# Later w1 loads, routing numbers in a PSUM bank and two more unsplit heads in a fused attention and mixture-of-experts kernel

## The chip, the cores and the metric

The kernel runs on one core of one Trainium2 chip. Its time is the device time of one execution in microseconds (us), lower is better. One execution was also taken by the hardware profiler; every row below comes from that one. The engines are TensorE (PE in the rows, PEld for its weight loads), VectorE (DVE), ScalarE (ACT), GpSimd (POOL) and the queue of SyncE (SPq), which issues most transfers.

## The reference, cut to what matters

Causal attention over 4 batches, 12 heads, 448 positions and head size 64 gives 1792 rows of 768 numbers; a router picks the best of 8 experts for each row, and that expert's two matrices are applied.

```python
scores = scale * np.matmul(q, k.transpose(0, 1, 3, 2))        # 4 x 12 x 448 x 448, causal mask
attn = softmax(scores); x = np.matmul(attn, v)                # x: 1792 x 768 after the heads are joined
logits = x @ w_gate + modality_bias[modality_id]              # 1792 x 8
e_idx = np.argmax(logits, axis=1)
gate_w = (exp(l) / (sum(exp(l)) + 1e-9))[e_idx]               # l = logits - their maximum
for e in range(8):
    out[mask_e] = gate_w[mask_e, None] * (relu(x[mask_e] @ w1[e]) @ w2[e])
```

## The kernel before

The program is written out in one order for all engines; each engine runs its own instructions in that order, and semaphores hold an instruction until what it needs is done. Attention is a loop `iteration(n)` over 48 heads (n = 0 to 47; 12 heads of a batch in three groups of 4), software-pipelined: iteration n computes the scores of head n on TensorE (`st_scores`), then transposes the probabilities of head n-2 (`st_trans`), then multiplies those of head n-3 with v (`st_pv`, into the PSUM bank `ot`), then joins a quarter of a finished group (`st_comb`, into the bank `x`). VectorE takes row minima and copies the scores (`p`, L274), computes the low half of the split probabilities (`pl`, L315), adds the two halves of the product (`ut`, L359) and normalises (L406, L416). ScalarE takes the exponentials (L284), the high half (`ph`, L314) and the low rows of the product (`hol`, L353).

Matrix products in full precision are made of fp32r products of high and low parts. For q and k the split is GpSimd's: `split_qk` (L191, L192) and `split_kl` (L197, L199) for a pair of heads, two heads at a time, and `stack_qk` has four transfers bring the parts on top of each other in a tile `st`. Heads 0 to 3 do without: `first_load` loads q and k of a pair into the tiles `raw1`, and `st_scores` multiplies them unsplit in fp32 (half as many matmuls, each of them slower). `raw1` is later the place where the first expert's w1 lands. GpSimd also splits v for each group (`split_vh`, `split_vl`, L238 and L243).

When the last group of a batch is normalised, `after_batch(b, n)` puts the router's small steps of that batch into the next iterations: the six steps `choose` (logits, maximum, difference, ties, choice), `places` (seven small matmuls, then two ScalarE copies, the second the exponential of the differences), the steps `rank`, and `scatter`, GpSimd's four indirect writes of the row numbers. `later(n, f)` puts f behind the scores of iteration n, `before(n, f)` ahead of them, and `soon(n, f)` behind the transposes. The batches end at iterations 19, 31, 43 and in the tail, so `choose` stands in iterations 20 to 23, 32 to 35, 44 to 47 and in the tail.

After batch 1 the most frequent expert is taken as the first one to be computed (`first_expert`, `first_slot`); its w1 is loaded in six chunks, chunk k in iteration 31 + `W1AT[k]`. GpSimd splits chunks 0 to 2 in iterations 45, 46 and 47. The experts follow after the attention; TensorE bounds that part almost alone.

In the names of PSUM tiles each bank is 128 x 512 fp32; of bank `ot` the attention uses columns 0 to 447.

Of the kernel before, what the change touches and what calls it, by code (L numbers as in the profile page):

```python
# [21 lines left out]
def attention_moe(  # L22
# [47 lines left out]
    ps = ctx.enter_context(tc.tile_pool(name="ps", bufs=1, space=PSUM))  # L70

    def bank(tag, bufs=1):
        return ps.tile([128, 512], F32, tag=tag, name=tag, bufs=bufs)

    def sm(shape, tag, dt=F32, bufs=2):
        return small.tile(shape, dt, tag=tag, name=tag, bufs=bufs)

    def cst(name, shape, dt=F32):
        return const.tile(shape, dt, name=name)
# [16 lines left out]
    lts = [ltp[:, j] for j in range(2)]  # L96
    sls = [cst(f"sl{j}", [128, NTL, E + 1]) for j in range(2)]
    ent = cst("ent", [128, B, NTL, 2], I32)
# [119 lines left out]
    def first_view(m, c):  # L218
        return raw1[3 * m + c][:, 0:S]

# [214 lines left out]
    def route(b):  # L435
        lg = sm([128, NTL, E], "lg")
        m = sm([128, NTL], "m")
        eq = sm([128, NTL, E], "eq")
        m2 = sm([128, NTL], "m2")
        oh = sm([128, NTL, E], "oh", BF16)  # L440
        pe = sm([128, NTL, E], "pe")
        pc = sm([128, NP + E], "pc")
# [23 lines left out]
        def places():  # L466
            prev = rt[b - 1][0][:, NP:] if b else ebase
            ohf = oh.rearrange("p t e -> p (t e)")
            pos = bank("x")
            nc.tensor.matmul(  # L470
                pos[:, 0:NP + E].rearrange("p (t e) -> p t e", e=E), lhsT=onesf,
                rhs=eb(prev, NTL + 1)[0:1], start=True, stop=False,
            )
            nc.tensor.matmul(pos[:, 0:NP], lhsT=upper, rhs=ohf, start=False, stop=False)
            for j in range(1, NTL + 1):
                nc.tensor.matmul(
                    pos[:, j * E:NP + E], lhsT=ones, rhs=ohf[:, 0:NP + E - j * E], start=False, stop=(j == NTL)
                )
            A.activation(out=pc, in_=pos[:, 0:NP + E], func=AF.Copy)
            A.activation(out=pe, in_=lg, func=AF.Exp)  # L480
            rt[b] = (pc, si)
# [7 lines left out]
        def ranks():  # L489
            V.tensor_reduce(out=sr, in_=sl, axis=AX, op=ALU.add)  # L490
            V.tensor_scalar(out=zs, in0=zs, scalar1=1e-9, scalar2=None, op0=ALU.add)

        def gates():
            V.tensor_copy(si, sr)
            V.reciprocal(out=ent[:, b, :, 1].bitcast(F32), in_=zs)
# [7 lines left out]

        sr = sm([128, NTL], "sr")
        return (logits, top, centre, ties, first_tie, choice), places, (slots, ranks, gates), scatter

    def eb(a, x):
        return a.rearrange("p (o e) -> p o e", o=1).to_broadcast([a.shape[0], x, E])
# [26 lines left out]
    def first_base():  # L535
        V.tensor_scalar(out=eboff, in0=ebneg, scalar1=now[:, 2:3], scalar2=None, op0=ALU.add)
        V.tensor_scalar(out=eb64, in0=ebneg, scalar1=now[:, 3:4], scalar2=None, op0=ALU.add)

# [17 lines left out]
    def first_tri():  # L556
        V.tensor_scalar(out=n0, in0=oh0, scalar1=-1.0, scalar2=1.0, op0=ALU.mult, op1=ALU.add)
        V.tensor_tensor(out=tri0, in0=ctri, in1=eb(n0, E), op=ALU.mult)

    def first_order():  # L560
        V.tensor_tensor(out=tri0, in0=tri0, in1=eb(oh0, E), op=ALU.add)
        V.tensor_tensor(out=tri0, in0=tri0, in1=n0.rearrange("p (e o) -> p e o", o=1).to_broadcast([128, E, E]), op=ALU.mult)

# [309 lines left out]
    with tc.manual_schedule():  # L873
        for m in range(2):
            first_load(m)
        load_v(0)
        load_qk(2)
        nc.sync.dma_start(out=modi, in_=mod)
# [10 lines left out]
        V.memset(warm, 0.0)  # L889
        for m in range(2):  # L890
            for a in range(2):
                V.memset(first_view(m, a)[64 - a * 64:128 - a * 64], 0.0)
        A.activation(out=warm, in_=warm, func=AF.Exp)
# [34 lines left out]
        for j in range(2):  # L928
            V.memset(sls[j], 0.0)
            V.memset(sls[j][64:128, 0, E:E + 1], 1.0e6)  # L930
            V.memset(lts[j][64:128, 0], 0.0)
# [68 lines left out]
        e0 = []  # L1000
        W1AT = (8, 9, 14, 14, 15, 15)

# [8 lines left out]
        def after_batch(b, n):  # L1011
# [6 lines left out]
            last = b == B - 2  # L1018
            soon(n + 4, places)
            for j, f in enumerate(rank, 1):  # L1020
                (later if j % 2 else before)(n + 5 + j // 2, f)
            for i in range(NTL):
# [42 lines left out]
        def iteration(n):  # L1065
            if n % 2 == 1 and n + 3 < NHEAD:
                stack_qk((n + 3) // 2)
            if n and n % GH == 0 and n // GH + 1 < B * NG:
                load_v(n // GH + 1)
# [18 lines left out]
            if n == 0:  # L1088
                split_vh(0)
                split_vl(0)  # L1090
                load_v(1)
            if n % 2 == 1 and n + 3 < NHEAD:
                split_kl((n + 3) // 2)
            if n % 2 == 0 and n + 4 < NHEAD:
                split_qk((n + 4) // 2)
# [310 lines left out]
```

## Time and profile before

| | |
|---|---|
| median of 3 runs | 507.45 us (507.43 to 509.28) |
| the profiled execution | 509.06 us, of it span 507.3 us |
| TensorE busy | 478.0 us (94%) |
| VectorE, ScalarE, GpSimd busy | 302.1, 279.4, 242.8 us |
| mean granted TensorE clock | 0.990 of full speed |
| attention (scores of heads 0 to 47) | about 4 to 204 us of the span |

The span runs from the first instruction to the last; the 1.8 us around it belong to the execution too. Busy time over the whole span mixes the attention, in which four engines are busy nearly all the time, with the experts, in which TensorE alone is.

### The profile page before, as it was taken

To read this page: it belongs to the slowest core of one execution; us is meant where nothing else is said; L and a number is where in the kernel's file an instruction comes from. 1 tells how busy PE (TensorE), PEld (TensorE's weight loads), DVE (VectorE), ACT (ScalarE), POOL (GpSimd) and SP (SyncE) were. 2 spreads that over 40 slices of the span, in tenths; PEclk is the share of its full clock that TensorE was granted. 3 is DMA by queue.
4 is the path that set the end of the run, shared out by engine and by line. 5 is a ranking of instruction groups with operands and counts; after the bars stand their busy time and mean duration, and the time that the engine had idled before them with its cause. 6 is when DMAs were issued, how large, how long until landed. Compare 5 with 4: busy or idle time off the path is not lost.

```text
span 507.3 us, 10362 instructions
## 1 busy us (share of the span) xinstructions
PE 478.0 (94%) x3359; PEld 442.8 (87%) x3359; DVE 302.1 (60%) x893; ACT 279.3 (55%) x690; POOL 242.8 (48%) x295
## 2 busy tenths in 40 slices
PE   8699999999989988899999999999999999999990
PEld 6589899899878977778999999999999999889770
DVE  7689888999899989888523015452021120184490
ACT  5499999899978977624322125442112211284670
POOL 5799999899999979952220202202101001021131
PEclk9899999999999999999999999999999999999997
DMA  5998788987997869765478300972101001076200
GB/s 149 210 237 212 181 229 239 285 223 188 243 263 222 199 124 270 248 164 71 96 265 328 96 32 21 323 281 66 63 1 54 31 2 64 31 261 214 88 14 6
DMA packets 44106, 79.84 MB, mean 157 GB/s; under 512 B 15614, under 2 KB 27646, under 8 KB 44032
## 3 DMA queue, kind: packets, MB, share of 16 engines
q1 hardware_dynamic: 40992, 67.98, 49.1%
q0 software_dynamic: 3040, 11.03, 6.3%
q8 instruction: 28, 0.46, 0.4%
q14 instruction: 46, 0.38, 0.2%
HBM read 48.10 MB, written 11.89 MB: 118 GB/s over the span
## 4 chain that ended last, share of the span: by engine, by line
PE 48%; POOL 16%; DVE 12%; DMA 11%; issue 6%; ACT 4%; SPq 1%; POOLq 0%; DVEq 0%; ACTq 0%
PE g L747 7%; PE g L748 7%; PE g L749 7%; DVE pl L315 3%; DVE p L274 2%; DMA table<-ent,si 2%; POOL hl L192 2%; DMA st<-hl 2%; POOL vhl L243 2%; PE ot L748 2%; PE ot L747 2%; PE x L749 2%; PE x L748 2%; PE x L747 2%; PE ot L749 2%
## 5 line engine op out<-in xcount | busy, mean ns | idle before, releaser
L284 ACT ACTIVATE p<-p,nm 128x448 f32<-128x448 f32 x192 | 94.8, 497 | 4.3 <-DVE nm L274 4.3
L728 POOL DMA_INDIRECT xg<-xs,idg x18 | 20.9, 1161 | 156.4 <-DVEq L1316 79.3
L766 DVE SCALAR_TENSOR_TENSOR htl<-g,hth 128x256 fp32r<-128x256 f32 x40 | 16.7, 424 | 103.8 <-ACT hth L765 103.8
L747 PE MATMUL g<-xh,w1h 128*128 128x256 f32 x240 | 67.1, 280 | 0.5 <-DVE htl L766 0.5
L748 PE MATMUL g<-xl,w1h 128*128 128x256 f32 x240 | 67.0, 279 | 0.0
L749 PE MATMUL g<-xh,w1l 128*128 128x256 f32 x240 | 67.0, 279 | 0.0
L296 PE MATMUL pt<-ident,p 128*128 128x128 f32 x432 | 64.2, 276 | 0.0
L315 DVE TENSOR_TENSOR pl<-pt,ph 128x1024 fp32r<-128x1024 f32 x48 | 58.3, 1214 | 7.4 <-ACT ph L314 6.5
L314 ACT ACTIVATE ph<-pt 128x1024 fp32r<-128x1024 f32 x48 | 48.9, 1019 | 13.1 <-PE pt L296 12.7
L328 PE MATMUL ot<-ph,vhl 128*128 128x448 f32 x192 | 50.3, 302 | 5.9 <-DVE ut L359 5.6
L296 PEld LDWEIGHTS pt<-ident,p 128*128 128x128 f32 x432 | 52.9, 149 | 0.8 <-issue 0.2
L765 ACT ACTIVATE hth<-g 128x256 fp32r<-128x256 f32 x40 | 15.1, 383 | 62.7 <-PE g L749 59.7
L747 PEld LDWEIGHTS g<-xh,w1h 128*128 128x128 f32 x240 | 45.1, 188 | 0.7 <-DVE htl L766 0.7
L749 PEld LDWEIGHTS g<-xh,w1l 128*128 128x128 f32 x240 | 45.1, 188 | 0.0
L748 PEld LDWEIGHTS g<-xl,w1h 128*128 128x128 f32 x240 | 45.1, 188 | 0.0
L807 POOL DMA_INDIRECT out_dram<-row,idg x14 | 16.0, 1141 | 60.0 <-ACTq L1300 33.5
L328 PEld LDWEIGHTS ot<-ph,vhl 128*128 128x128 f32 x192 | 33.0, 191 | 9.5 <-DVE ut L359 8.1
L274 DVE CUSTOM_DVE_ANT_0 p<-sa,mask 128x448 f32<-128x448 f32 x96 | 36.2, 413 | 6.0 <-PE sa L265 5.5
L274 DVE CUSTOM_DVE_ANT_0 p<-sb,mask 128x192 f32<-128x192 f32 x96 | 36.3, 412 | 0.1
L284 ACT ACTIVATION_READ_ACCUMULATOR p<-p,nm 128x1 f32 x192 | 36.3, 189 | 0.0
L335 PE MATMUL ot<-pl,vhl 128*64 128x64 f32 x192 | 34.4, 294 | 0.0
L353 ACT ACTIVATE hol<-ot 64x448 f32<-64x448 f32 x48 | 26.0, 541 | 13.4 <-PE ot L328 8.5
(347 smaller groups left out, 1346.6 us busy)
## 6 DMA issues: line engine op xcount, KB each, us to landing
st<-hl SPq DMA_DIRECT2D x60, 224.0 KB
raw<-in_moe_w_dram SPq DMA_DIRECT2D x24, 512.0 KB
raw<-in_qk_dram SPq DMA_DIRECT2D x22, 448.0 KB
raw<-in_moe_w_dram SPq DMA_DIRECT2D x20, 384.0 KB
vraw<-in_v_dram SPq DMA_DIRECT2D x12, 384.0 KB
xs<-row SPq DMA_DIRECT2D x12, 384.0 KB
w1h<-hl SPq DMA_DIRECT2D x14, 224.0 KB
w1l<-hl SPq DMA_DIRECT2D x14, 224.0 KB
```

The source lines that it names most:

```text
L274: V.tensor_tensor_reduce(out=z, in0=o, in1=m, scale=-scale, scalar=3.0e38, op0=ALU.add, op1=ALU.min, accum_out=nm[:n, i:i + 1],)
L284: A.activation(out=z, in_=z, func=AF.Exp, bias=nm[:n, i:i + 1], scale=-1.0, accum_out=sums[:n, b, i, h:h + 1],)
L296: nc.tensor.transpose(out=o, in_=a, identity=ident)
L314: A.activation(out=ph, in_=t, func=AF.Copy)
L315: V.tensor_tensor(out=pl, in0=t, in1=ph.bitcast(F32), op=ALU.subtract)
L328: nc.tensor.matmul(o[:, q0:S], lhsT=t[:rows, kt, h].rearrange("p a d -> p (a d)"), rhs=ph[:rows, c0:c1], start=(n == 0), stop=(n == 1),)
L335: nc.tensor.matmul(o[0:D, q0:S], lhsT=t[:rows, kt, h, 0], rhs=pl[:rows, c0:c1], start=False, stop=False)
L353: A.activation(out=t, in_=ov[g][64:128, :S], func=AF.Copy)
L728: P.indirect_dma_start(out=xg[u][:n], out_offset=None, in_=xs[0:rows, :], in_offset=bass.IndirectOffsetOnAxis(ap=g[:n, 0:1], axis=0), boun ...
L747: nc.tensor.matmul(o, lhsT=ah, rhs=bh, start=first, stop=False)
L748: nc.tensor.matmul(o, lhsT=ah, rhs=bl, start=False, stop=False)
L749: nc.tensor.matmul(o, lhsT=al, rhs=bh, start=False, stop=last)
```

## The change

It has these parts:

1. Heads 4 and 5 are loaded with `first_load(2)` and multiplied unsplit, like heads 0 to 3, in the second half of the columns of `raw1[0]` to `raw1[2]`. The splits and stacking transfers of that pair go, two memsets of 64 x 448 on GpSimd come. `load_v(1)` is issued in iteration 1, after the load of the pair of heads 6 and 7.
2. The tile `ot` becomes one tile `otb` for the whole kernel, and the router's logits and ties stand in its columns 448 to 511.
3. `places` and `rank` stand one iteration later. Two of the six small steps of `rank` go: the sum over experts plus a cast becomes a maximum with an integer result, and the 1e-9 comes from a ninth column that is set once.
4. `first_base` moves from VectorE to ScalarE (three small activations), and `first_tri` and `first_order` from VectorE to GpSimd (three small multiplications and additions).
5. `W1AT` goes from (8, 9, 14, 14, 15, 15) to (11, 13, 14, 14, 15, 15).

```diff
+    otb = ps.tile([128, 512], F32, name="otb")
     def bank(tag, bufs=1):
+        if tag == "ot":
+            return otb
...
-        return raw1[3 * m + c][:, 0:S]
+        k = 3 * m + c
+        return raw1[k % K1][:, k // K1 * S:k // K1 * S + S]
...
     def route(b):
-        lg = sm([128, NTL, E], "lg")
+        lg, eq = (otb[:, S + j * NTL * E:S + (j + 1) * NTL * E].rearrange("p (t e) -> p t e", e=E) for j in range(2))
...
         def ranks():
-            V.tensor_reduce(out=sr, in_=sl, axis=AX, op=ALU.add)
-            V.tensor_scalar(out=zs, in0=zs, scalar1=1e-9, scalar2=None, op0=ALU.add)
-
-        def gates():
-            V.tensor_copy(si, sr)
+            V.tensor_reduce(out=si, in_=sl, axis=AX, op=ALU.max)
             V.reciprocal(out=ent[:, b, :, 1].bitcast(F32), in_=zs)
...
     def first_base():
-        V.tensor_scalar(out=eboff, in0=ebneg, scalar1=now[:, 2:3], scalar2=None, op0=ALU.add)
-        V.tensor_scalar(out=eb64, in0=ebneg, scalar1=now[:, 3:4], scalar2=None, op0=ALU.add)
+        A.activation(out=eboff, in_=ebneg, func=AF.Identity, bias=now[:, 2:3])
+        A.activation(out=eb64, in_=ebneg, func=AF.Identity, bias=now[:, 3:4])
+        A.activation(out=n0, in_=oh0, func=AF.Copy, scale=-1.0, bias=1.0)
...
-        load_qk(2)
+        first_load(2)
...
-        W1AT = (8, 9, 14, 14, 15, 15)
+        W1AT = (11, 13, 14, 14, 15, 15)
...
-            soon(n + 4, places)
+            soon(n + 5, places)
             for j, f in enumerate(rank, 1):
-                (later if j % 2 else before)(n + 5 + j // 2, f)
+                (later if j % 2 else before)(n + 6 + j // 2, f)
...
-            if n % 2 == 1 and n + 3 < NHEAD:
+            if n % 2 == 1 and 5 < n + 3 < NHEAD:
                 stack_qk((n + 3) // 2)
+            if n == 1:
+                load_v(1)
```

Three places show what moves. First GpSimd from its first split of v on (`vhl` of group 0), before:

```order
L238 TENSOR_SCALAR vhl<-vraw 128x16x64
L243 TENSOR_TENSOR vhl<-vraw,vhl 128x16x64
L191 TENSOR_SCALAR hl<-raw 128x896
L192 TENSOR_TENSOR hl<-raw,hl 128x448
L197 TENSOR_TENSOR xh<-raw,hl 128x448
L199 TENSOR_SCALAR qz_151<-raw,half 128x448 x2
L191 TENSOR_SCALAR hl<-raw 128x896
L192 TENSOR_TENSOR hl<-raw,hl 128x448
L238 TENSOR_SCALAR vhl<-vraw 128x16x64
L243 TENSOR_TENSOR vhl<-vraw,vhl 128x16x64
```

and the same place after the change (line numbers of the changed file):

```order
L243 TENSOR_SCALAR vhl<-vraw 128x16x64
L248 TENSOR_TENSOR vhl<-vraw,vhl 128x16x64
L195 TENSOR_SCALAR hl<-raw 128x896
L196 TENSOR_TENSOR hl<-raw,hl 128x448
L243 TENSOR_SCALAR vhl<-vraw 128x16x64
L248 TENSOR_TENSOR vhl<-vraw,vhl 128x16x64
```

The first four split instructions for q and k (pair 2: heads 4 and 5, five instructions in all) are gone, so that the first split is that of pair 3, with the v of group 1 right behind it.

Second TensorE in iteration 20, at the end of the transposes of head 18 and the start of the product of head 17; in square brackets stand the semaphores that an instruction waits for. Before:

```order
L296 MATMUL pt<-ident,p_2_154 128x128
L296 MATMUL pt<-ident,p_3_155 128x128
L328 MATMUL ot<-ph,vhl 128x448 [waits DVE_49]
L328 MATMUL ot<-ph,vhl 128x192
L335 MATMUL ot<-pl,vhl 64x64
L335 MATMUL ot<-pl,vhl 64x448
```

and after the change:

```order
L301 MATMUL pt<-ident,p_2_157 128x128
L301 MATMUL pt<-ident,p_3_158 128x128
L333 MATMUL otb<-ph,vhl 128x448 [waits DVE_49,Activation_49]
L333 MATMUL otb<-ph,vhl 128x192
L340 MATMUL otb<-pl,vhl 64x64
L340 MATMUL otb<-pl,vhl 64x448
```

The counts of these semaphores in the built programs say which instruction is meant: before, VectorE's `ut` (L359) of head 16, the last reader of the bank; after, VectorE's logits (L452 in the changed file), which stand behind the minima of head 20, and ScalarE's `hol` of head 16. In iterations 21, 22 and 23 the product waits in the same way for the difference (L458), the maximum of the ties (L464) and the choice (L467), in iteration 24 for ScalarE's exponential (L484). It is so in every batch but the last, in 14 iterations of the loop and one of the tail; in the other iterations the wait is for `ut` as before.

Third SyncE's queue from iteration 39 to 41; `raw_112` and `raw_113` are the tiles `raw1[0]` and `raw1[1]`. Before:

```order
L680 TENSOR_LOAD sch_106
L663 ISA
L663 DMA raw_112<-in_moe_w_dram 128x1024
L231 DMA vraw<-in_v_dram 128x3x256
L232 DMA vraw<-in_v_dram 64x256
L663 ISA
L663 DMA raw_113<-in_moe_w_dram 128x1024
L186 DMA raw<-in_qk_dram 128x896
L208 DMA st_165<-hl 64x896
L209 DMA st_165<-hl 64x2x448
```

After the change the two loads of w1 stand behind the stores of finished rows (`xs`) and the reads of the routing tables (`idq`), around the stacking transfers of heads 46 and 47; this is the part from the first to the second of them:

```order
L433 DMA xs<-row 128x768
L212 DMA st_169<-hl 64x896
L213 DMA st_169<-hl 64x2x448
L212 DMA st_169<-hl 64x896
L213 DMA st_169<-hl 64x2x448
L433 DMA xs<-row 128x768
L662 ISA
L662 DMA raw_116<-in_moe_w_dram 128x1024
```

So the stacking transfers of heads 44 and 45 (`st_165` above) and the load of q and k of heads 46 and 47 ahead of them no longer follow two loads of 512 KB.

## Rows read from the trace of the kernel before

**Rows 1.** TensorE's timeline around heads 3 to 6: start, length, instruction, idle before it.

```profile
14.41 0.92 PE L265 MATMUL sa<-raw,raw 128*128 128x448 f32 x2
...
16.24 0.70 PE L328 MATMUL ot<-ph,vhl 128*128 128x448 f32 x2
...
21.98 0.44 PE L265 MATMUL sa<-st 128*128 128x448 f32 x1 [4.34 <-DMA st<-hl]
...
26.89 0.36 PE L265 MATMUL sa<-st 128*128 128x448 f32 x1
...
27.95 0.71 PE L296 MATMUL pt<-ident,p 128*128 128x128 f32 x5
...
30.11 0.37 PE L265 MATMUL sa<-w1h 128*128 128x448 f32 x1
```

**Rows 2.** Stretches: length, busy time of each engine, granted clock, DMA share, GB/s.

```profile
22.00:25.60 3.60, 3.60 (x19) 3.53 (x20) 2.60 (x10) 0.00 (x0) 3.52 (x3) 0.59 1.00 228
84.85:105.93 21.08, 20.44 (x164) 18.70 (x163) 20.30 (x67) 18.49 (x55) 18.76 (x24) 1.00 1.01 264
132.75:155.73 22.98, 20.70 (x163) 18.73 (x163) 20.84 (x67) 18.46 (x55) 22.24 (x27) 1.00 0.91 255
155.73:168.72 12.99, 12.29 (x96) 10.80 (x95) 12.76 (x44) 11.63 (x34) 12.05 (x16) 1.00 0.69 187
168.72:186.22 17.50, 15.79 (x125) 14.61 (x125) 17.16 (x54) 16.12 (x50) 13.75 (x18) 1.00 0.91 194
186.22:206.18 19.96, 17.03 (x132) 14.97 (x132) 18.25 (x57) 13.64 (x39) 19.15 (x22) 1.00 0.84 242
```

**Rows 3.** TensorE's timeline in iterations 30 to 32.

```profile
125.00 0.46 PE L265 MATMUL sa<-w1h 128*128 128x448 f32 x1
...
127.23 0.54 PE L328 MATMUL ot<-ph,vhl 128*128 128x448 f32 x2
...
128.71 0.47 PE L265 MATMUL sa<-w1l 128*128 128x448 f32 x1
...
132.75 0.47 PE L265 MATMUL sa<-st 128*128 128x448 f32 x1
```

**Rows 4.** GpSimd's timeline at its first splits of q and k.

```profile
12.43 0.93 POOL L191 TENSOR_SCALAR hl<-raw 128x896 fp32r<-128x896 f32 x1
...
15.66 1.27 POOL L199 TENSOR_SCALAR qz<-raw,half 128x448 fp32r<-128x448 f32 x2
20.24 0.94 POOL L191 TENSOR_SCALAR hl<-raw 128x896 fp32r<-128x896 f32 x1 [3.31 <-DMA raw<-in_qk_dram]
```

**Rows 5.** The chain that ended last, in order of time, at the start.

```profile
4.90 3.87 DMA vraw<-in_v_dram
...
14.75 7.09 DMA st<-hl
```

**Rows 6.** VectorE's timeline: logits of batches 0 and 1, minima of head 40, a normalisation.

```profile
88.61 0.96 DVE L448 TENSOR_REDUCE lg<-ltp 128x32 f32<-128x416 f32 x1 [0.45 <-POOL ltp L406]
...
137.78 0.93 DVE L448 TENSOR_REDUCE lg<-ltp 128x32 f32<-128x416 f32 x1 [1.73 <-POOL ltp L406]
...
171.38 0.48 DVE L274 CUSTOM_DVE_ANT_0 p<-sb,mask 128x320 f32<-128x320 f32 x1
...
188.84 0.42 DVE L416 TENSOR_TENSOR row<-x,rec 64x256 f32<-64x256 f32 x1 [1.50 <-DMA xs<-row]
```

**Rows 7.** VectorE's small steps by line: shortest, median and longest in ns.

```profile
L454 DVE TENSOR_TENSOR lg<-lg,m x4: 191/1016/1509, 92.9 to 223.4; 128x32 f32<-128x32 f32 x4
L491 DVE TENSOR_SCALAR zs<-zs x4: 159/593/1017, 107.8 to 226.2; 128x4 f32<-128x4 f32 x4
```

**Rows 8.** The end of the attention: GpSimd's and TensorE's waits, and the first load of w1.

```profile
170.28 0.36 SPq L663 DMA_DIRECT2D raw<-in_moe_w_dram  x1
...
184.43 0.98 POOL L191 TENSOR_SCALAR hl<-raw 128x896 fp32r<-128x896 f32 x1 [3.01 <-issue]
...
186.22 0.44 PE L265 MATMUL sa<-st 128*128 128x448 f32 x1 [1.28 <-DMA st<-hl]
```

More of the change, by code (lines that the diff above doesn't have):

```diff
@@ L96, in attention_moe @@
     lts = [ltp[:, j] for j in range(2)]
-    sls = [cst(f"sl{j}", [128, NTL, E + 1]) for j in range(2)]
+    sls, pes = ([cst(f"{x}{j}", [128, NTL, E + 1]) for j in range(2)] for x in ("sl", "pe"))
     ent = cst("ent", [128, B, NTL, 2], I32)
@@ L435, in route @@
     def route(b):
-        lg = sm([128, NTL, E], "lg")
+        lg, eq = (otb[:, S + j * NTL * E:S + (j + 1) * NTL * E].rearrange("p (t e) -> p t e", e=E) for j in range(2))
         m = sm([128, NTL], "m")
-        eq = sm([128, NTL, E], "eq")
         m2 = sm([128, NTL], "m2")
         oh = sm([128, NTL, E], "oh", BF16)
-        pe = sm([128, NTL, E], "pe")
+        pe = pes[b % 2]
         pc = sm([128, NP + E], "pc")
@@ L479, in places @@
             A.activation(out=pc, in_=pos[:, 0:NP + E], func=AF.Copy)
-            A.activation(out=pe, in_=lg, func=AF.Exp)
+            A.activation(out=pe[:, :, 0:E], in_=lg, func=AF.Exp)
             rt[b] = (pc, si)
@@ L502, in scatter @@
                 )
-        sr = sm([128, NTL], "sr")
-        return (logits, top, centre, ties, first_tie, choice), places, (slots, ranks, gates), scatter
+        return (logits, top, centre, ties, first_tie, choice), places, (slots, ranks), scatter
     def eb(a, x):
@@ L556, in first_tri @@
     def first_tri():
-        V.tensor_scalar(out=n0, in0=oh0, scalar1=-1.0, scalar2=1.0, op0=ALU.mult, op1=ALU.add)
-        V.tensor_tensor(out=tri0, in0=ctri, in1=eb(n0, E), op=ALU.mult)
+        P.tensor_tensor(out=tri0, in0=ctri, in1=eb(n0, E), op=ALU.mult)
     def first_order():
-        V.tensor_tensor(out=tri0, in0=tri0, in1=eb(oh0, E), op=ALU.add)
-        V.tensor_tensor(out=tri0, in0=tri0, in1=n0.rearrange("p (e o) -> p e o", o=1).to_broadcast([128, E, E]), op=ALU.mult)
+        P.tensor_tensor(out=tri0, in0=tri0, in1=eb(oh0, E), op=ALU.add)
+        P.tensor_tensor(out=tri0, in0=tri0, in1=n0.rearrange("p (e o) -> p e o", o=1).to_broadcast([128, E, E]), op=ALU.mult)
     def schedule_a(cnt):
@@ L889, in attention_moe @@
         V.memset(warm, 0.0)
-        for m in range(2):
+        for m in range(3):
             for a in range(2):
-                V.memset(first_view(m, a)[64 - a * 64:128 - a * 64], 0.0)
+                (P if m == 2 else V).memset(first_view(m, a)[64 - a * 64:128 - a * 64], 0.0)
         A.activation(out=warm, in_=warm, func=AF.Exp)
@@ L929, in attention_moe @@
             V.memset(sls[j], 0.0)
+            V.memset(pes[j], 1e-9)
             V.memset(sls[j][64:128, 0, E:E + 1], 1.0e6)
@@ L1090, in iteration @@
                 split_vl(0)
-                load_v(1)
-            if n % 2 == 1 and n + 3 < NHEAD:
+            if n % 2 == 1 and 5 < n + 3 < NHEAD:
                 split_kl((n + 3) // 2)
-            if n % 2 == 0 and n + 4 < NHEAD:
+            if n % 2 == 0 and 5 < n + 4 < NHEAD:
                 split_qk((n + 4) // 2)
```

## The prediction

> **What bounds the kernel now.** I read the busy time by slices first: it says where the engines share the work. In the experts TensorE is alone and never waits for long, so whatever the attention loses or gains moves the end by as much. In the attention I read windows from the scores of one head to those of a later one. In 84.85 to 105.93 (heads 20 to 25) TensorE is busy 20.44 of 21.08 us, VectorE 20.30, GpSimd 18.49 and ScalarE 18.76 [rows 2]: no engine alone is the bound, and a wait on any of them is paid by the next.
>
> The least that a head takes I read from TensorE's timeline where nothing holds it: 125.00 to 128.71 is 3.71 us, the fourth head of a group (128.71 to 132.75) 4.04 us; the product starts 2.23 us after the scores (127.23) and the next scores 1.48 us after that [rows 3]. So four heads take 15.17 us at least and heads 20 to 25 18.88 (the fourth head among them once). Over this least the windows lose 2.2 us (heads 20 to 25), 4.1 (32 to 37: 22.98), 1.5 (37 to 40: 12.99 against 11.46), 2.3 (40 to 44: 17.50) and 4.8 (44 to the tail: 19.96) [rows 2]. These are the router's iterations, which the change rewrites.
>
> Then the start, by the chain that ended last and the timelines of TensorE and GpSimd: head 4 begins at 21.98 after an idle 4.34 us, for its stacking transfers [rows 1], which land 7.09 us after 14.75 [rows 5], since GpSimd's splits for that pair run from 12.43 to 16.93 [rows 4].
>
> **Part 1, heads 4 and 5: a gain.** Unsplit scores take 1.83 us (14.41 to 16.24), split ones 1.06 (26.89 to 27.95), so each of the two heads pays 0.77 us. An iteration there takes 3.22 us (26.89 to 30.11), with unsplit scores 3.99 [rows 1]. Head 4 needs only its load, so it starts when head 3 is done: 21.98 less 4.34, some 17.6. Head 6 then starts at 17.6 + 2 x 3.99 = 25.6 instead of 30.11: 4.5 us less. This counts the slow clock behind the stop: it was 0.59 of full speed, near the lower of its two levels (1.2 of 2.4 GHz), in 22.00 to 25.60 [rows 2], and head 4 took 4.91 us (21.98 to 26.89) for 3.22 [rows 1].
>
> What could eat it: head 6's own splits. The first of them started at 20.24 after 3.31 us for its load [rows 4]; now 4.5 us of splits ahead of it are gone and its load stands earlier in the queue. If it starts by 14, its splits (4.5 us) and a landing of 7.09 us [rows 5] end by 25.6, just in time. The two memsets (estimated at 0.4 us each from the 0.93 us of a split over twice the columns and both halves [rows 4]) lie in GpSimd's idle time until v lands (4.90 + 3.87 = 8.77 [rows 5]). I take −4.4. Bounds: −4.7 if head 3 also runs freer, and −2.2 if v of group 1 and the stack land late and half of the stop comes back.
>
> **Part 2, the PSUM columns: a gain on VectorE, a wait on TensorE.** A step of 128x32 between two tiles of SBUF takes 191 ns at the best and 1509 at the worst, the 1e-9 step on 128x4 159 to 1017 ns [rows 7]. The long ones lie beside GpSimd's splits. With the logits in PSUM the step has one SBUF operand. By the Trainium skill ("SBUF — State Buffer", "Who interferes with whom") a VectorE operation with at most one SBUF input outside the two-port modes doesn't contend with GpSimd. By that rule the steps would fall to their shortest; the rows' spread agrees, but none shows such a step in PSUM. So the difference takes 0.8 us less (1016 to 191), and the 1e-9 step that goes gives 0.6. VectorE gains this, the end only where a window loses time to VectorE; there I count it below.
>
> The price is in the order: in iteration 20 the first product waits for the logits, since both are in one tile's bank. Before, the logits ended at 88.61 + 0.96 = 89.57 [rows 6]; the product of head 17 could start at 84.85 [rows 2] + 2.23 = 87.08. TensorE so stops for 2.5 us. Queued behind it are the scores of head 21, for which VectorE and ScalarE wait. The Trainium skill ("PSUM — Partial Sum Buffer", "PSUM bank collisions raise a hardware error") has PSUM guarded by bank and quadrant, not by address, which is why the order shows waits between columns that don't overlap; that speaks against this part.
>
> In iteration 21 the product waits for the difference, which is short: +0.5. In 22 it waits for the maximum of the ties, behind the minima: those of head 40 end 171.86 [rows 6], 3.14 us after that head's scores (168.72 [rows 2]), against 2.23 for the product. That is up to 0.9, and with the step itself (0.2) 1.1; a normalisation ahead of it can add 0.42 [rows 6]. I take +1.2. In 23 nothing: the choice stands an iteration ahead. In 24 `places` stands in the old path, and its exponential is waited for: +0.9, between nothing and the 1.0 us of iteration 22.
>
> Heads 20 to 25 would so take 18.88 + 2.5 + 0.5 + 1.2 + 0.9 = 24.0 us instead of 21.08: **+3.0**. Bounds: +0.5 (the logits' stop alone, 18.88 + 2.5 = 21.4, rounded up by a wait of 0.2) and +3.5.
>
> In batch 1 the logits come 5.06 us after the scores (137.78 − 132.75), of which 1.73 is GpSimd's lag [rows 2, 6]. The splits gone at the start leave GpSimd ahead, so I count that wait as gone; the rest as in batch 0, 23.65 against 22.98, +0.7. The next window loses the stretched steps of `rank` (0.6 of its 1.5). Together **+0.1**, between −1.5 and +2.
>
> **Parts 3 to 5, the end of the attention: a gain.** In 168.72 to 186.22 two loads of w1 go. The first is issued at 170.28, ahead of the stacks and of the last load of q and k; TensorE waits 1.28 us for the stack of head 44, GpSimd 3.01 for that load [rows 8] and VectorE 1.50 for a transfer of finished rows [rows 6]. The loss of that window is 2.3; I take 1.9 of it, since six small steps less on VectorE leave room too. The same steps on GpSimd (three, about 0.9 by the 0.93 of the larger split [rows 4]) and ScalarE (three, some 0.6) lie in idle time: GpSimd is busy 16.12 of 17.50, ScalarE 13.75 [rows 2]. Were that cover gone, they cost 0.9. The moved loads land two iterations ahead of their splits. From head 44 on 4.8 us are lost already; the wait for the logits of batch 2 replaces one for the same chain: −0.45. `places` one step later in the tail costs +0.5. Together **−1.85**, between −3 and +1.
>
> **Sum.** −4.4 + 3.0 + 0.1 − 1.85 = −3.15. The span of 507.3 us becomes 504.1 and the profiled execution, 509.06, 505.9. The median of the runs is 1.6 lower than that execution: 507.45 − 3.15 = 504.3; I say **504.2**. A difference of 0.5% (2.54 us) is about what a measurement of this kernel can tell from no change.
>
> **The rivals.**
> - *Only the wait for the logits costs* (0.25). VectorE, relieved of its long steps, is ahead when the other steps come, and the product finds them done. For it: a step without GpSimd beside it takes 191 ns [rows 7]. Against it: the minima of a head end after the product could start [rows 6], and a step put behind them can't be earlier. A batch would take 18.88 + 2.5 + 0.2 = 21.6: +0.5 and −1.4; the window after batch 1 gives −0.6, that of heads 40 to 44 −1.9, and the last takes 15.17 + 2.7 for 19.96, −2.1. With −4.4 that is −9.9: 497.5.
> - *The change gives little where it should* (0.15). The stack of head 6 is the next late one (7.09 us to land [rows 5]) and half of the start's gain goes; the moved w1 loads meet the stacks of heads 46 and 47 and the stores of rows, so the waits of 1.28 and 1.50 only move. Then −2.2 + 3.0 + 0.1 − 0.7 = +0.2: 507.6, no change.
> - *The stops slow the clock* (0.08), the other side. After an idle of 4.34 us the granted clock was 0.59 [rows 1, 2]; a stop of 2.5 us may do the same. A slow iteration cost 4.91 − 3.22 = 1.7 us [rows 1]; two behind each of three stops are +10: 514. It makes the kernel slower by over 0.5% from +5.7 us, some 1.1 slow iterations for each stop. Against it: 1.00 in all five windows of the router's iterations, which hold stops too, if shorter ones [rows 2]. The Trainium skill ("TensorE: Matmul & The Clock Gate", "What's actually happening") has the throttled clock as the default, which activity lifts to 2.4 GHz from 1.2.
>
> **How the numbers follow.** The sum's own case has 0.52, with a range of 502 to 506.5. The four cases put 0.25 around 497.5, 0.15 near 507.5 and 0.08 above 510. Range 497 to 508.5: it leaves out the lower half of the first rival, the third and the edge of the second. Faster by over 0.5% (below 504.9): nearly all of the first rival and 0.33 of the sum's case, 0.58; within 0.5%: the rest of it and the second rival, 0.34; slower (above 510.0): 0.08.
>
> **What the profile after would show.** Head 4 at some 17.6 without a wait for a transfer, head 6 at 25 to 26. In iterations 20, 32 and 44 an idle of TensorE of 2 to 2.5 us ahead of the product, ended by VectorE's logits, and lesser ones in the two behind; the difference at about 0.19 us; heads 20 to 25 in 23.6 to 24.1. Scores of head 44 with no wait for the stack. A granted clock of 1.00 through the loop. Wrong would make it: a clock under 1.00 behind those stops; waits of the product of 1 us and more in every one of the five iterations (then the sum is above 507), or none (then it is the first rival); head 6 waiting for its stack at 27 or later.

## The result and the profile after

The changed kernel takes 513.83 us (median of 4 runs, 512.65 to 514.93), the kernel before 507.44 beside it: 1.0123 of before, 95% interval 1.0091 to 1.0154. It is slower by 6.4 us where 3.2 us less were forecast, and outside the range. The profiled execution took 513.35 us, its span is 511.6 us instead of 507.3. The spans differ by less than the medians (4.3 us), since the profiled execution of the kernel before was 1.6 us above its median.

The page of the changed kernel: span, TensorE's row (busy time, share, instructions) and its granted clock in 40 slices, in tenths.

```profile
span 511.6 us, 10351 instructions
PE 480.7 (94%) x3359; PEld 446.5 (87%) x3359; DVE 292.1 (57%) x881; ACT 279.7 (55%) x693; POOL 240.8 (47%) x295
PEclk9999998999899989999999999999999999999996
```

VectorE does 10 us less, and the kernel is slower: its busy time was not the price. The clock row has three places under full speed ahead of the last slice: two behind the product's stops at the logits of batches 0 and 1, the third behind TensorE's wait for the stack of head 44 (all three stops are shown below). The stretches of [rows 2] again, by windows of the changed kernel (length; busy time of PE, PEld, DVE, ACT, POOL; granted clock, DMA share, GB/s): heads 20 to 25, a piece of that, heads 32 to 37, 37 to 40, 40 to 44, 44 to the tail's transposes, and a piece of head 44.

```profile
80.38:105.61 25.23, 21.87 (x163) 20.27 (x163) 19.34 (x65) 18.46 (x55) 21.74 (x26) 0.93 0.92 248
86.00:88.90 2.90, 2.90 (x14) 2.77 (x13) 1.58 (x6) 2.33 (x9) 2.82 (x5) 0.50 1.07 367
132.24:157.93 25.69, 21.86 (x163) 20.14 (x163) 19.32 (x65) 18.31 (x55) 23.91 (x29) 0.93 0.86 242
157.93:169.83 11.90, 11.89 (x96) 10.84 (x95) 11.67 (x44) 11.63 (x34) 8.21 (x11) 1.00 0.50 135
169.83:187.74 17.91, 15.44 (x125) 14.54 (x125) 15.63 (x50) 17.25 (x54) 15.51 (x21) 1.00 0.73 141
187.74:210.42 22.68, 17.99 (x132) 16.52 (x132) 15.95 (x57) 12.76 (x34) 19.21 (x24) 0.92 0.87 265
188.00:191.00 3.00, 3.00 (x15) 2.86 (x15) 0.57 (x2) 0.00 (x0) 2.92 (x2) 0.50 0.91 249
```

Set against [rows 2] (and the starts of the stretches), this is the sum of the prediction with what the trace shows:

| stretch | forecast | shown |
|---|---|---|
| start to head 20 (84.85 to 80.38) | −4.4 | −4.47 |
| heads 20 to 25 (21.08 to 25.23) | +3.0 | +4.15 |
| heads 25 to 32 (26.82 to 26.63) | 0 | −0.19 |
| heads 32 to 40 (22.98 + 12.99 to 25.69 + 11.90) | +0.1 | +1.62 |
| head 40 to the tail (17.50 + 19.96 to 17.91 + 22.68) | −1.85 | +3.13 |
| the rest (301.12 to 301.18) | 0 | +0.06 |
| span | −3.15 | +4.30 |

TensorE's timeline at heads 4 and 6, then its idle times of more than 1.2 us between head 6 and the tail's transposes:

```profile
17.61 0.54 PE L270 MATMUL sa<-raw,raw 128*128 128x448 f32 x1
...
26.06 0.37 PE L270 MATMUL sa<-w1h 128*128 128x448 f32 x1
...
84.67 0.44 PE L333 MATMUL otb<-ph,vhl 128*128 128x448 f32 x1 [1.80 <-DVE otb L452]
...
137.09 0.71 PE L333 MATMUL otb<-ph,vhl 128*128 128x448 f32 x1 [2.37 <-DVE otb L452]
...
187.74 0.53 PE L270 MATMUL sa<-st 128*128 128x448 f32 x1 [2.47 <-DMA st<-hl]
...
193.31 0.44 PE L333 MATMUL otb<-ph,vhl 128*128 128x448 f32 x1 [1.50 <-DVE otb L452]
...
209.96 0.27 PE L474 MATMUL x<-pc,onesf 1*128 1x40 f32 x1 [1.96 <-DVE row L421]
```

Against [rows 1], heads 4 and 6 come as forecast. Then come the three logits (L452), as forecast too. Not forecast are the longer wait for the stack of head 44 (2.47 for 1.28 in [rows 8]) and a stop ahead of `places` in the tail (L474, for the bank `x` that VectorE's normalisation still reads). On VectorE, two of the logits, the wait for its row buffer in iteration 44, and the difference as a group (count, busy, mean ns):

```profile
83.62 0.90 DVE L452 TENSOR_REDUCE otb<-ltp 128x32 f32<-128x416 f32 x1
...
136.04 0.91 DVE L452 TENSOR_REDUCE otb<-ltp 128x32 f32<-128x416 f32 x1 [0.50 <-POOL ltp L411]
...
190.43 0.42 DVE L421 TENSOR_TENSOR row<-x,rec 64x256 f32<-64x256 f32 x1 [3.34 <-DMA xs<-row]
```

```profile
L458 DVE TENSOR_TENSOR otb<-otb,m 128x32 f32<-128x32 f32 x4 | 0.8, 190 | 0.0
```

The difference takes about 190 ns in every batch (933 in the mean before; [rows 7] has its spread). On GpSimd there is a wait that the prediction doesn't have, ahead of the first indirect write of batch 1 (`scatter`); `xf` is VectorE's next step behind the two that make the numbers of this write:

```profile
164.57 1.00 POOL L499 DMA_INDIRECT table<-ent,si  x1 [2.27 <-DVE xf L524]
```

### The profile page after: what moved, and what is told of

It is laid out like the page before. It is cut to its first block, busy times and chain, and to the rows that moved or that the text cites. A ratio compares the mean times of both kernels' runs of the same rounds, so it can differ in the third digit from the quotient of the medians.

```text
span 511.6 us, 10351 instructions
## 1 busy us (share of the span) xinstructions
PE 480.7 (94%) x3359; PEld 446.5 (87%) x3359; DVE 292.1 (57%) x881; ACT 279.7 (55%) x693; POOL 240.8 (47%) x295
## 4 chain that ended last, share of the span: by engine, by line
PE 51%; POOL 22%; DVE 8%; issue 7%; DMA 7%; ACT 2%; SPq 1%; POOLq 0%; DVEq 0%; ACTq 0%
PE g L746 7%; PE g L748 7%; PE g L747 7%; POOL vhl L248 3%; POOL qz L203 3%; POOL hl L196 3%; POOL hl L195 2%; DMA raw<-in_qk_dram 2%; POOL xh L201 2%; PE otb L748 2%; PE otb L747 2%; PE x L748 2%; PE x L747 2%; PE x L746 2%; PE otb L746 2%
## 5 line engine op out<-in xcount | busy, mean ns | idle before, releaser
L333 PE MATMUL otb<-ph,vhl 128*128 128x448 f32 x192 | 50.5, 304 | 11.5 <-DVE otb L452 5.7
L333 PEld LDWEIGHTS otb<-ph,vhl 128*128 128x128 f32 x192 | 33.3, 193 | 14.7 <-ACT ph L319 6.2
L358 ACT ACTIVATE hol<-otb 64x448 f32<-64x448 f32 x48 | 26.0, 543 | 20.3 <-PE otb L333 19.1
L340 PE MATMUL otb<-pl,vhl 128*64 128x64 f32 x192 | 35.0, 297 | 0.0
```

Source lines behind the costliest of these rows:

```text
L333: nc.tensor.matmul(o[:, q0:S], lhsT=t[:rows, kt, h].rearrange("p a d -> p (a d)"), rhs=ph[:rows, c0:c1], start=(n == 0), stop=(n == 1),)
L340: nc.tensor.matmul(o[0:D, q0:S], lhsT=t[:rows, kt, h, 0], rhs=pl[:rows, c0:c1], start=False, stop=False)
L358: A.activation(out=t, in_=ov[g][64:128, :S], func=AF.Copy)
```

## The experiments

All were timed beside the kernel before, whose median there was 508.7 to 509.6 us; so the ratios are compared, not the times. The theory at the start: the stops behind the bank and the half clock behind them are the loss, with the waits at the end of the attention. The rival: the loss is in the steps that were moved.

**Part 1 alone** (kernel before, with the edits of `first_load`, its tiles and memsets, `load_v` and the conditions on the pairs).

> The kernel before with part 1 alone (heads 4 and 5 unsplit, v of group 1 issued in iteration 1). Theory: the gain of the start, 4.5 us at head 20 in the changed kernel (80.38 against 84.85), stays to the end: 503.0 us. Rival: the waits at the end of the attention (stack of head 44, stores of rows) don't come earlier with it and take it back: 505 to 507.5.

Measured 502.46 us, 0.9884 of before (0.9859 to 0.9910), so some 5.9 us less; its span is 499.7 us. The gain stays to the end and grows (4.55 us at head 20, 7.6 at the end of the profiled execution). The theory holds, and the size is over the forecast.

**Logits and ties back in SBUF**, all else as changed:

```diff
-        lg, eq = (otb[:, S + j * NTL * E:S + (j + 1) * NTL * E].rearrange(...) for j in range(2))
+        lg, eq = (sm([128, NTL, E], x) for x in ("lg", "eq"))
```

> The changed kernel with logits and ties in SBUF tiles again, all else as changed. Theory: the stops of the product behind VectorE's logits (1.80, 2.37 and 1.50 us) and the half clock behind them go, heads 20 to 25 take 21 us instead of 25.2 and heads 32 to 37 some 23 instead of 25.7; the small steps are stretched again (about 1 us): 505 to 506. Rival: the loss is with what moved around them (places, rank, scatter, w1): no less than 511.

Measured 506.83 us (504.01 to 511.11), 0.9974 of before (0.9948 to 1.0000). So the columns are the larger part of the loss, and parts 3 to 5 still eat most of part 1's gain (0.9884 alone). Both theory and rival have a share.

**The columns alone**, in the kernel before (`otb` for bank `ot`, `lg` and `eq` in it):

> The kernel before with one tile for the bank of the product and logits and ties in its columns 448 to 511, nothing else. Theory: three stops of 1.5 to 2.4 us at the logits, half clock behind two or three of them, lesser waits behind: 1.010 to 1.016 of before. Rival: most of the loss of the changed kernel is from the other parts, and the relief of VectorE pays for the waits: 1.000 to 1.004.

Measured 519.09 us, 1.0216 (1.0184 to 1.0248): 11 us. Windows of this kernel for heads 20 to 25, 32 to 37 and 44 to 47, and the last of these in the kernel before:

```profile
85.39:109.76 24.37, 20.44 (x164) 18.79 (x163) 19.27 (x67) 18.47 (x55) 20.26 (x26) 1.00 0.97 246
136.78:160.75 23.97, 20.43 (x164) 18.78 (x163) 19.11 (x67) 18.47 (x55) 23.21 (x28) 1.00 0.88 241
191.22:209.19 17.97, 13.42 (x95) 12.51 (x94) 14.50 (x47) 10.63 (x32) 13.92 (x16) 0.91 0.72 212
```

```profile
186.22:199.78 13.56, 12.00 (x93) 10.94 (x94) 12.00 (x39) 9.31 (x26) 13.07 (x15) 1.00 0.77 201
```

In this execution the clock stayed at full speed in the first two, and they cost +3.3 and +1.0 against [rows 2], close to the forecast of +3.0 and +0.7. The third costs +4.4, where −0.45 was forecast (for all parts together). Its stop at the logits is 3.50 us, and the clock of the window is 0.91. VectorE comes late to these logits by its own work: it has no pause of 0.2 us between 180 and 198 us, and a step of `first_order`, which this kernel leaves on VectorE, takes 1.54 us there:

```profile
197.20 0.44 PE L332 MATMUL otb<-ph,vhl 128*128 128x448 f32 x1 [3.50 <-DVE otb L451]
```

```profile
190.75 1.54 DVE L564 TENSOR_TENSOR tri<-tri,oh 128x64 f32<-128x64 f32 x1
```

**The columns for batches 0 and 1 only** (SBUF tiles from batch 2 on):

> The kernel before with the columns for the logits and ties of batches 0 and 1, and SBUF for batches 2 and 3. With the columns for all it measured 1.0216. Theory: heads 20 to 25 lose 3.3 us and 32 to 37 about 1, as there; the end of the attention, where the columns cost 4.4 more from head 44 to 47, is as before: 1.008 to 1.011. Rival: the loss of the first two batches makes the end late by itself, or is caught up there: 1.02, or under 1.005.

Measured 514.04 us, 1.0096 (1.0077 to 1.0115). So of the 11 us about 5 belong to the first two batches and 6 to the third and the tail, as expected. Its window for heads 20 to 25 has the clock at 0.93, and is 1.36 us longer than the first row above, with the same instructions on TensorE:

```profile
84.78:110.51 25.73, 21.90 (x163) 20.28 (x163) 19.41 (x67) 18.54 (x55) 22.24 (x28) 0.93 0.95 240
```

**The clock by itself**: the stops stay, but TensorE works in them.

```diff
+    def fill_pe(g, count):
+        t = ahead[g] = pair_bank()
+        for j in range(count):
+            c = 128 * (j % 4)
+            nc.tensor.transpose(out=t[:, c:c + 128], in_=ident, identity=ident)
...
+            if n in (20, 32):
+                fill_pe(n - 1, 13)
```

> The changed kernel with 13 transposes of the identity put on TensorE in iterations 20 and 32, between the transposes and the product, into the bank that the next head's transposes overwrite; the product's wait stays. Theory: the clock stays at 1.00 behind the two stops, and 1.3 us each are saved: 511. Rival: the stop itself is all the cost and the clock's share is hidden behind VectorE and ScalarE: 513.8, or more if the transposes outlast the wait.

Measured 512.41 us, 1.0086 (1.0057 to 1.0115). The two windows of the filled iterations:

```profile
80.54:104.35 23.81, 21.86 (x177) 20.20 (x176) 19.16 (x65) 18.32 (x55) 21.67 (x26) 1.00 0.94 256
130.97:155.35 24.38, 21.85 (x177) 20.20 (x176) 19.24 (x65) 18.32 (x55) 23.64 (x29) 1.00 0.88 243
```

They are 1.42 and 1.31 us shorter than 25.23 and 25.69 in the changed kernel, and the clock is 1.00. Heads 20 to 25 have full clock without any filler too, for one in the changed kernel with the loads of w1 undone (below), which has the same instructions up to iteration 39 and a stop of 1.79 us there:

```profile
80.28:104.07 23.79, 20.43 (x163) 18.77 (x163) 19.16 (x65) 18.32 (x55) 21.77 (x26) 1.00 0.99 263
```

This is 1.44 us shorter than 25.23. So a slow stretch (some 3 us at half clock behind a stop) costs 1.3 to 1.4 us, with the stop as it is. That the filler is what kept the clock up is not shown: in batch 0 the clock also stayed up without it, and in batch 1, where three profiles without it have 0.93 behind stops of 2.36 to 2.38 us, there is only this one with it. In the total the difference (1.9 us) is within the intervals; the windows carry the price.

**Another slot for the same steps**: two of the six at a time, behind `ut` and ahead of the minima. The logits so come later in the program (at the head of iteration 21, not behind the minima of head 20), but directly behind the instruction that frees the bank. The texts below call these the earlier slots.

```diff
-                (later if j % 2 else before)(n + 1 + j // 2, f)
+                before(n + 2 + (j - 1) // 2, f)
```

> The changed kernel with the six steps of the choice two by two behind VectorE's sum of the product (ut) in iterations n+2 to n+4, ahead of the minima; the logits stay in the PSUM columns. Theory: the product no longer waits for a step that stands behind the minima, so the stops and the half clock behind them go; as with the logits in SBUF, 0.995 to 0.998 of before. Rival: any use of the bank by VectorE between two products costs: 1.008 or slower.

Measured 504.34 us, 0.9909 (0.9875 to 0.9943): 11 us less than the changed kernel, with the logits in the same columns. Heads 20 to 25 and 32 to 37, then the wait that is left behind the logits of batch 0 (in batch 1 it is 0.67 us too), and one in batch 2:

```profile
79.83:100.92 21.09, 20.04 (x163) 18.75 (x163) 19.35 (x65) 18.36 (x55) 19.57 (x25) 1.00 1.03 265
127.54:148.64 21.10, 20.05 (x163) 18.76 (x163) 19.35 (x65) 18.35 (x55) 20.43 (x25) 1.00 0.90 255
```

```profile
86.70 0.44 PE L333 MATMUL otb<-ph,vhl 128*128 128x448 f32 x1 [0.67 <-DVE m L455]
...
193.37 0.44 PE L333 MATMUL otb<-ph,vhl 128*128 128x448 f32 x1 [2.33 <-DVE otb L461]
```

The rival, that any use of the bank costs 1.008 or more, falls. In batches 0 and 1 the stops came from where the steps stood: behind the minima of a head whose scores TensorE had just made, ahead of a product that was ready. In batch 2 the bank still stops TensorE: in iteration 46 VectorE waits 2.26 us for its row buffer between `ut` and the pair of steps with the ties (L461), and the product waits for the ties.

**The moved loads of w1**, once undone in the changed kernel (`W1AT` from 8, 9) and once alone on top of part 1:

> The changed kernel with the two loads of w1 in iterations 39 and 40 again, as before. Theory: VectorE's wait of 3.34 us for the store of rows and what follows it go, 2 to 4 us less than the changed kernel: 1.005 of before. Rival: the loads then hold up the stack of head 44 and its q and k as before: 1.012 or slower.

> The kernel before with part 1 and part 5 alone (heads 4 and 5 unsplit; the first two loads of w1 in iterations 42 and 44). Part 1 alone measured 0.988 of before. Theory: the first load, issued right behind a store of finished rows, makes that store land late; VectorE waits some 3 us for its row buffer, TensorE stops and its clock falls, and GpSimd waits for w1 later: 3 to 5 us more than part 1 alone, 0.995 to 0.998 of before. Rival (the prediction's): the loads leave the way of the stacks and give 1 to 2 us: 0.985.

Undone: 514.20 us, 1.0130 (1.0092 to 1.0168), the same as the changed kernel. Alone: 505.21 us, 0.9917 (0.9892 to 0.9943) beside 0.9884 for part 1; the intervals overlap, so a loss of some 1.7 us isn't certain, but no gain is there. With the loads back in iterations 39 and 40 TensorE waits 3.36 us for the stack of head 44, with them away from it 2.47: the stack was late in both. My theory of the stores is not borne out (VectorE's wait for its row buffer is 3.49 us with the loads undone), nor is the prediction's gain.

**The writes of batch 1** one iteration later in the changed kernel:

```diff
-                later(n + 7 + (2 * i, i // 2, 0)[b], lambda i=i: scatter([i]))
+                later(n + 7 + (2 * i, 1 + i // 2, 0)[b], lambda i=i: scatter([i]))
```

> The changed kernel with the four indirect writes of batch 1 one iteration later. Theory: GpSimd's wait of 2.27 us for VectorE ahead of the first of them goes, the splits of heads 42 to 45 come 2 us earlier, and the wait of 2.47 us for the stack of head 44 falls under 1: 511 to 512. Rival: GpSimd is ahead there anyway, and the stack lands no earlier: 513.8.

Measured 512.07 us, 1.0060 (1.0040 to 1.0080), about 3 us less than the changed kernel. Head 44 comes without a wait for its stack:

```profile
184.49 0.47 PE L270 MATMUL sa<-st 128*128 128x448 f32 x1
```

Heads 40 to 44 take 15.45 us there (169.04 to 184.49) instead of 17.91. The stack was late since GpSimd's splits were, and these since GpSimd stood at a write whose numbers VectorE made an iteration later than before.

**The shift of `places` and `rank` alone**, on top of part 1 (`soon(n + 5, places)`, rank from n + 6):

> The kernel before with part 1, and places and the steps of rank one iteration later (of part 3 the shift alone). Part 1 alone measured 0.988 of before. Theory: the writes of batch 1 stay in iteration 38, now the one in which VectorE ends rank, so GpSimd waits some 2 us for VectorE, its splits and the stack of head 44 come later by as much, and 2 to 3 us are lost: 0.993 of before. Rival: VectorE is early enough without the columns: 0.988.

Measured 512.54 us, 1.0075 (1.0054 to 1.0096): it costs 9.7 us, far more than either forecast. Three waits of this kernel, on GpSimd, VectorE and TensorE, and the clock from head 44 on and behind the last of them:

```profile
160.65 1.00 POOL L500 DMA_INDIRECT table<-ent,si  x1 [3.63 <-DVE ent L496]
...
187.37 0.42 DVE L417 TENSOR_TENSOR row<-x,rec 64x256 f32<-64x256 f32 x1 [3.49 <-DMA xs<-row]
...
206.30 0.40 PE L471 MATMUL x<-pc,onesf 1*128 1x40 f32 x1 [3.80 <-DVE row L417]
```

```profile
184.73:190.04 5.31, 5.31 (x32) 5.17 (x32) 2.67 (x12) 1.17 (x2) 5.23 (x6) 0.68 0.54 143
206.30:213.97 7.67, 7.67 (x47) 7.51 (x48) 2.13 (x4) 3.63 (x12) 3.57 (x3) 0.60 0.51 170
```

TensorE had waited 2.64 us for the stack ahead of the first of these windows. The second is slow for about twice as long as the first. Counted as three slow stretches at 1.3 to 1.4 us, they come to some 4 of the 9.7 us, an estimate. Part 1 alone has no such place in its loop.

Two kernels take this apart. In the first the writes of batch 1 are moved along (the edit above); in the second batch 2 keeps the old place (`late = b < B - 2` in place of the 1).

> The kernel before with part 1, places and rank one iteration later, and the writes of batch 1 one iteration later too. Without the last it measured 1.0075 of before, part 1 alone 0.988. Theory: GpSimd's wait of 3.63 us for VectorE goes, the stack of head 44 comes earlier; 3 to 5 us of the 9.7 are given back: 0.998 to 1.002. Rival: all of the loss is the stop ahead of places in the tail: 1.007.

> The kernel before with part 1, and places and rank one iteration later in batches 0 and 1 alone; in batch 2 they stay in iteration 47 instead of the tail. Theory: TensorE's wait of 3.80 us ahead of places in the tail and the half clock behind it go, 4 to 5 us: 0.998. The wait of GpSimd stays. Rival: the stop in the tail stands for work that is late anyway: 1.007.

Measured 510.19 us, 1.0032 (1.0016 to 1.0049), and 508.22 us, 0.9995 (0.9978 to 1.0012). So the writes carry about 2 us and `places` in the tail about 4. The remaining 3 to 4 are not told apart: each of the two kernels keeps the other's wait, and none has both edits. The clock changes with them: each of these two profiles has one slow stretch, the one above three.

**The losses mended together.** The changed kernel with the earlier slots, the later writes and w1 as before; the same with the logits in SBUF; the first with batch 2's `places` in iteration 47 again; and parts 1 and 2 with the earlier slots alone, in PSUM and in SBUF.

> The changed kernel with the choice two by two ahead of the minima, the writes of batch 1 one iteration later, and the first two loads of w1 in iterations 39 and 40 again. Theory: the three losses found are gone, and the rest of the change stays: 0.982 to 0.986 of before. Rival: the later places and rank still cost in the tail: no faster than part 1 alone, 0.988 or more.

> The changed kernel with choice in the earlier slots, the later writes and the earlier loads of w1 (0.9855 of before), and logits and ties in SBUF. Theory: the relief of VectorE is hidden, and what is left of the columns is a wait for ScalarE's exponential: 0.984 to 0.986. Rival: three stretched steps ahead of the minima in each batch: 0.988.

> The changed kernel with choice in the earlier slots, the later writes and the earlier loads of w1 (0.9855 of before), and places and rank of batch 2 in iteration 47 again instead of the tail. Theory: TensorE's wait of 1.95 us ahead of places in the tail goes, 1 to 2 us: 0.982 to 0.984. Rival: places then waits for VectorE's choice in iteration 47, as in the kernel before (1.36 us), and the product behind it for ScalarE's exponential: 0.986 or more.

> The kernel before with part 1, the logits and ties in PSUM columns, and the six steps of the choice two by two ahead of the minima; places, rank, first_base and w1 as before. Theory: no stop of the product for these steps, and VectorE's steps at 0.19 us: 1 to 3 us less than part 1 alone, 0.982 to 0.986 of before. Rival: the columns cost in any slot: 0.990 or slower.

> The same with logits and ties in SBUF (two tiles as before). Theory: the difference, ties and choice are stretched beside GpSimd to 0.46 to 1.0 us each and stand ahead of the minima, 0.5 to 1 us per batch slower than with the columns: 0.986 to 0.989 of before. Rival: the slots alone do it and the columns give nothing: the same time as with the columns within 0.5 us.

| kernel | us | of before |
|---|---|---|
| mended | 501.17 | 0.9855 (0.9829 to 0.9880) |
| mended, logits in SBUF | 505.59 | 0.9937 (0.9923 to 0.9951) |
| mended, batch 2 as before | 500.52 | 0.9837 (0.9802 to 0.9872) |
| parts 1 and 2, earlier slots | 503.75 | 0.9906 (0.9883 to 0.9929) |
| the same, logits in SBUF | 501.53 | 0.9857 (0.9833 to 0.9880) |

The third is the fastest kernel here, faster than both given ones; from the first, and from part 1 alone (0.9884), its interval doesn't part it. What the columns give is open. In the mended kernel they are worth 4 us, in the other pair they cost 2, and in that pair heads 20 to 25 differ little; the totals part at the end of the attention. Of the last two, heads 20 to 25 and then head 44, with the columns:

```profile
80.15:101.23 21.08, 20.03 (x163) 18.75 (x163) 19.33 (x67) 18.48 (x55) 19.99 (x26) 1.00 1.00 272
181.09:187.80 6.71, 6.71 (x32) 6.49 (x32) 3.00 (x12) 1.34 (x2) 6.63 (x9) 0.52 0.60 151
```

and in SBUF:

```profile
80.03:100.81 20.78, 20.38 (x163) 18.58 (x163) 19.98 (x67) 18.48 (x55) 18.93 (x23) 1.00 1.01 268
180.00:184.38 4.38, 3.95 (x32) 3.65 (x32) 4.35 (x14) 3.09 (x10) 4.30 (x5) 1.00 0.41 82
```

With the columns TensorE had waited 2.95 us for the stack of head 44, in SBUF 0.32. In the mended kernel the two part in the tail: ahead of `places` TensorE waits 1.95 us with the columns, at full clock, and 3.69 in SBUF, with a clock of 0.74 behind it (200.23 to 206.71). So in both pairs the slower kernel has the longer stop, with a slow stretch behind it, and the other has none; that the columns bring this about, one profile of each doesn't show.

## Why the prediction was wrong

**Part 1 was right** in place, mechanism and size up to head 20 (−4.47 for −4.4). It gave more in the end when left alone (0.9884), since heads 32 to 37 are shorter too (21.41 us from 128.68 to 150.09, for 22.98), and heads 40 to 44. GpSimd is ahead there by the splits that went: VectorE's wait of 1.73 us for it at the logits of batch 1 [rows 6] is gone.

**Part 2, batches 0 and 1.** The mechanism was right: the product waits for the logits, then in 22 for the step behind the minima and in 24 for the exponential. The sizes were, too, at full clock. In the window of 23.79 us above, heads 20 to 24 take 2.0, 0.6, 1.0, 0.0 and 1.2 us over their least (starts at 80.28, 86.01, 90.36, 95.10, 99.14, 104.07), where 2.5, 0.5, 1.2, 0 and 0.9 were forecast. The rule of the Trainium skill ("PSUM — Partial Sum Buffer", "PSUM bank collisions raise a hardware error") that speaks against the part names what is to be guarded, bank and quadrant; the traces agree in that waits stand between columns that don't overlap. The step that failed is the weight of the third rival: "the stops slow the clock", with a chance of 0.08. Behind the stops of 1.80 and 2.37 us the granted clock fell to 0.50 for some 3 us each time (86.00 to 88.90 above), which the prediction had named as a sign of being wrong. Its price was over-sized in the rival: 3.4 us for a stop, where the runs show 1.3 to 1.4. That its total of 514 lies beside the measured 513.83 is luck: by that price the three slow stretches of the trace make some 4 us of its 10 (an estimate), one of them behind another stop, and nearly all the rest of the miss is at the end of the attention. I had weighed stops of 1.6 us and less in the trace of before, with a clock of 1.00, as evidence for longer ones. In batch 1 a second step failed: "I count that wait as gone". GpSimd's part of the logits still came last (0.50 us, at 136.04), 3.8 us after the scores instead of 5.03, and the stop was 2.37.

**The end of the attention** is the largest miss, +3.13 for −1.85. A slow stretch is in it (188.00 to 191.00 above, behind the wait for the stack of head 44), and three steps of the prediction failed:
- "The first is issued at 170.28, ahead of the stacks and of the last load of q and k; TensorE waits 1.28 us for the stack": the loads stood there, but moving them gave nothing, alone or undone. Standing behind a transfer in a queue was taken for waiting on it.
- "`places` one step later in the tail costs +0.5": about 4 us in the kernel with part 1. In the tail it stands ahead of the transposes and needs the bank `x`, which VectorE's normalisation frees, itself behind the minima of head 47, the low half and `ut`: TensorE stops for 1.96 us in the changed kernel, 3.80 in the other, in which a choice stretched to 1.75 us stands there too.
- The writes of batch 1 were not in the sum at all. They stayed in iteration 38, while the numbers they need moved there from 37. GpSimd's queue was the one I didn't follow past the moved step; it cost 2 to 3 us, by way of the stack of head 44 and the slow stretch behind it.

The logits of batch 2 were put at −0.45 since they "replace" a wait of the same chain. With the columns alone they, and the tail, cost 6 us (1.0216 less 1.0096). VectorE is late at head 44 there: its minima begin 3.4 us after the head's scores (194.66 and 191.22), those of head 20 1.9 us (87.25 and 85.39), and the bank made TensorE wait for all that stood ahead of the logits. Before, the product needed only `ut`, which stands ahead of them. In the changed kernel, which has `first_order` on GpSimd, VectorE waits 3.34 us for its row buffer instead.

The parts don't add: part 1 and the columns alone measure −5.9 and +11, the shift and the loads of w1 on top of part 1 +9.7 and 0 to +1.7, and all together +6.4. A likely reason, not shown, is that several delay the same last iterations, so that part of each is hidden behind the others. Part 4 and the steps that `rank` lost were not run by themselves; what they give is open.

**The relief of VectorE** was right as forecast: the difference fell to 190 ns. The rule of the Trainium skill ("SBUF — State Buffer", "Who interferes with whom") agrees with that. It pays only where VectorE sets the pace, and the three batches inside the loop lost more at the bank than it gave; in the tail of the mended kernel, where TensorE waits 1.95 us ahead of `places` with the columns and 3.69 without, it may be what the 4 us there come from.

**Slips that decide nothing.** The columns of [rows 2] are TensorE, its weight loads, VectorE, ScalarE, GpSimd. So in heads 20 to 25 ScalarE is busy 18.49 us and GpSimd 18.76, and in 168.72 to 186.22 ScalarE 16.12 and GpSimd 13.75; the prediction has both pairs the other way round. Its 5.06 us (137.78 − 132.75) is 5.03, 24.0 less 21.08 is 2.9, and the terms that it names for batch 1 give some 23.5 us, not 23.65.

## What to carry to other kernels

A small result put into free columns of a bank that TensorE cycles through makes TensorE wait for everything that stands ahead of that result on its engine; put its steps directly behind the bank's own reader, with nothing in between that can itself wait. Here that left 0.67 us of each of two stops, and 2.33 us where a wait for a store stood in between. When a step moves by an iteration, look for who uses its result in a queue that did not move, here GpSimd's writes, and for the shared bank at its new place. At the end of a pipelined stretch, price a wait by what stands ahead of it there, not by its size in the middle, and read the granted clock behind every stop: here a slow stretch cost 1.3 to 1.4 us on top of a stop of 1.8.

## What the runs showed of the hardware that was not expected

In the changed kernel the granted clock fell to 0.50, the lower of its two levels (1.2 of 2.4 GHz), behind a stop of 1.80 us of a TensorE that had been busy without a pause from 76 us on. It did so not at once but about a microsecond after the work went on (0.50 in 86.00 to 88.90 behind a stop that ended at 84.67). Windows of the changed kernel from the end of that stop to the first of these:

```profile
84.67:85.00 0.33, 0.33 (x2) 0.32 (x3) 0.33 (x1) 0.00 (x0) 0.33 (x2) 1.00 1.14 291
85.00:86.00 1.00, 1.00 (x9) 0.99 (x8) 0.64 (x1) 0.00 (x0) 1.00 (x3) 0.78 1.02 305
```

It doesn't do so in every execution. In heads 20 to 25 the clock stayed at 1.00 behind 1.79 us in the same instructions (23.79 us) and behind 2.36 us with the columns alone (24.37), and the window fell to 0.93 behind 2.29 us with the same instructions on TensorE (25.73). That may be why single runs of these kernels spread by 2 to 7 us. With transposes run in the stop, to no other use, it stayed at 1.00 in the one profile taken.
